# An MLP with SiLU and its gradients on one core: the last stores waited for on GpSimd, the first loads ahead of the entry barrier's arrival, and a warm-up that reads one broadcast column

## The chip, the cores and the metric

The kernel runs on one core of one Trainium2 chip. Times are device microseconds (us) of single executions. The span is the time from the first to the last instruction in the trace; the time was 1.7 to 1.9 us longer than the span in every run, and what fills that difference lies outside the trace. No run of this study was marked slow (the granted clock listed for each is 0.999 or 1.0), so all runs are compared.

## The reference

An MLP with SiLU, and its gradients; bfloat16 in and out, S = 2048, D = 640, F = 1536.

```python
def _fwd_reference(x, w1, w2):
    h = jnp.einsum("bsd,df->bsf", x, w1)
    h = _silu(h)
    return jnp.einsum("bsf,fd->bsd", h, w2)

def reference(x, w1, w2, grad_out):
    _out, _vjp = jax.vjp(_f, x, w1, w2)      # _f: _fwd_reference
    _grads = _vjp(grad_out)
    return (_out, *_grads)                   # out, grad x, grad w1, grad w2
```

## The kernel before

Six matmul stages follow each other on TensorE. The change touches only the two ends of the program.

At the start, each engine arrives at an entry barrier (a drain that adds to a semaphore), and then waits for GpSimd's release. A hook that edits the instruction list at the end of the build moves the first instructions between the arrival and the wait, so that they don't wait for the barrier:

```python
def start_before_entry_wait(nc, names):
    def move(nc):
        ...
            gate = next(
                k for k, i in enumerate(entry)
                if i.engine == engine and isinstance(i, mybir.InstEventSemaphore)
            )
            ...
            for i in reversed(moved):
                entry.insert(gate, i)
    nc.at_finalize(move)
```

Those instructions are a memset, 18 warm-up matmuls on the tile it fills, and the first loads. `x_nat` goes through ten TensorE transposes; `w1_nat` arrives in five row blocks of 384 KB (the first in two halves, one issued by SyncE and one by ScalarE), and the first matmuls consume it in that order. Warm-up matmuls are there because TensorE starts at half clock here: in the profile below, matmuls of 256 columns start 213 ns apart until 5.67 us and 109 ns apart after it. With 4 warm-up matmuls instead of 19, they became fast at 8.49 us instead of 4.33 (one profile each, in the experiments).

```python
NWARM = 18
...
warm = cpool.tile([P, P], dt_in, name="warm")
early = [nc.vector.memset(warm[:], 1.0)]
...
for i in range(NWARM):
    early.append(nc.tensor.matmul(wp[:, 0:P], lhsT=warm[:], rhs=warm[:], start=True, stop=True))
ident = cpool.tile([P, P], dt_in, name="ident")
make_identity(nc, ident[:])                       # on GpSimd, for the transposes
...
early += [load_x(nc.sync, 0), load_x(nc.scalar, 1)]
early += [load_w1(0, slice(0, F // 2)), load_w1(0, slice(F // 2, F), nc.scalar)]
early += [load_w1(k) for k in range(1, 3)]
for k in range(3, DT):
    load_w1(k)
...
def h_first(xT, aT, ghT):                         # the first stage
    pe_x(xT)                                      # ten transposes and their copies
    ...
    for dt_ in range(DT):                         # row block dt_ of w1: 12 matmuls of 256 columns
        for pair in range(NPAIR):
            h_pair_mm(hs[0][pair], pair, dt_, xT, halves[0])
    ...                                           # then 60 more for the second half of the columns
```

At the end, the last tile of the gradient of w1 is computed and stored in two pieces (384 and 128 columns), and another hook makes SyncE's wait for the last store the last of its waits:

```python
def wait_for_last_store_last(nc, name):
    def move(nc):
        ...
        late = [w for w in waits if w.id in lanes]
        waits = late + [w for w in waits if w.id not in lanes]
        end[at] = copy.replace(end[at], sync_info=mybir.SyncInfo(on_wait=waits, on_update=[]))
    nc.at_finalize(move)
```

After this wait, the exit sequence follows: all engines arrive, GpSimd gathers and releases them, GpSimd drains, clears the semaphores and drains, all arrive again, and GpSimd gathers and releases a second time.

## Time and profile before

| | before |
|---|---|
| time, median of 3 runs (range) | 320.86 us (320.43 to 321.17) |
| span of the profiled run | 318.9 us |
| last of the first loads that TensorE waits for ends | 7.69 us |
| last update of the last store, to the end of the span | 0.775 us |

First, the page of the profile: the busy line (share of the span), and the chain of work that ended last.

```profile
PE 314.2 (99%) x1516; PEld 150.7 (47%) x1544; DVE 102.7 (32%) x182; ACT 76.8 (24%) x139; POOL 0.7 (0%) x6
...
PE 96%; DMA 2%; issue 1%; SPq 0%; DVE 0%; DVEq 0%
PE hp L302 32%; PE hp L286 16%; PE hp L391 16%; PE hp L440 15%; PE hp L204 12%; PE hp L233 3%; DMA w_nat<-in_w_dram 2%; PE hp L421 1%; SPq L173 0%; SPq L170 0%; DVE g L432 0%; DVEq L432 0%; SPq L468 0%
```

TensorE is the bound, and only the load of w1 stands beside it in the chain, with 2%.

Second, the timeline of the first 8 us. Its columns are start and length in us, engine (SPq and ACTq are the sequencers that issue DMAs), line, operation and count; the bracket is idle time before the group and what ended it.

```profile
0.09 0.39 SPq L170 DMA_DIRECT2D x_nat<-in_x_dram  x1
0.21 0.38 ACTq L170 DMA_DIRECT2D x_nat<-in_x_dram  x1
...
0.28 0.17 DVE L143 MEMSET warm<- 128x128 bf16 x1 [0.28 <-issue]
...
0.50 2.10 PE L147 MATMUL wp<-warm 128*128 128x128 bf16 x18 [0.50 <-DVE warm L143]
0.54 2.31 SPq L173 DMA_DIRECT2D w_nat<-in_w_dram  x5
0.62 0.45 ACTq L173 DMA_DIRECT2D w_nat<-in_w_dram  x1
...
2.59 1.25 PE L195 MATMUL tp<-ident,x_nat 128*128 128x128 bf16 x10
...
3.79 4.45 PE L233 MATMUL hp<-xT,w_nat 128*128 128x256 bf16 x27
5.00 0.88 PEld L233 LDWEIGHTS <-w_nat 128*128 128x128 bf16 x6 [0.25 <-DMA w_nat<-in_w_dram]
6.18 1.21 PEld L233 LDWEIGHTS <-w_nat 128*128 128x128 bf16 x12 [0.30 <-DMA w_nat<-in_w_dram]
...
7.73 0.33 PEld L233 LDWEIGHTS <-w_nat 128*128 128x128 bf16 x4 [0.35 <-DMA w_nat<-in_w_dram]
```

TensorE's weight loader (PEld) waits for w1 three times, 0.25 to 0.35 us each, and not again after 7.73 us. The matmuls lose less by it: the first of these waits delays none of them, and the other two make one matmul each late, by 0.18 us at 6.18 us and by 0.23 us at 7.74 us (gaps between starts of 294 and 342 ns instead of 109).

Third, how fast TensorE runs in that stretch: three windows of 1.5 us, with TensorE's busy time, the number of matmuls, the granted clock, the DMA engines' share and GB/s.

```profile
5.00:6.50 1.50, 1.48 (x11) 1.00 0.84 287
6.50:8.00 1.50, 1.43 (x14) 1.00 1.08 387
8.00:9.50 1.50, 1.50 (x17) 1.00 1.07 189
```

A matmul of 256 columns starts every 213 ns at half clock and every 109 ns at full clock, so 7 or 14 of them start in a full window; the count also takes in those that are still running at its edges. The clock column says 1.00 throughout, although the starts are 213 ns apart until 5.67 us: the clock record in the trace file begins only where full clock is granted, at 5.66 us here, and the column takes what lies before it for full clock.

Fourth, the sequencers' instructions at the end, listed by source line (minimum, median and maximum ns; first and last start).

```profile
L479 POOLq DRAIN  x3: 34/78/386, 1.0 to 318.7; - x3
L479 SPq DRAIN  x3: 7/7/13, 318.2 to 318.5; - x3
...
L479 PEldq EVENT_SEMAPHORE  x2: 51/51/51, 318.4 to 318.9; - x2
L479 POOLq EVENT_SEMAPHORE_RANGE_CLEAR  x1: 96/96/96, 318.5 to 318.5; - x1
```

Apart from GpSimd's first drain, at 1.0 us, the instructions in these lines start after the last store has landed, at 318.15 us. The trace's record of instructions and semaphore updates gives the order:

```
318.147  last update of the last store's semaphore
318.164  SyncE drain (its wait for that store is over)
318.233  SyncE drain, arrives at the exit barrier
318.265  GpSimd gathers          318.344  GpSimd releases
318.429  GpSimd drain (78 ns)    318.536  GpSimd clears the semaphores (96 ns)    318.661  GpSimd drain (34 ns)
318.739  GpSimd gathers          318.818  GpSimd releases
318.871  TensorE's last wait, 51 ns: end of the span at 318.922
```

### The profile page before, as it was taken

How to read it: one execution, taken by the hardware profiler on the slowest of the kernel's cores; microseconds unless marked ns; L12 is line 12 of the kernel's file. 1: busy time of each engine (PE TensorE's matmuls, PEld its weight loads, DVE VectorE, ACT ScalarE, POOL GpSimd, SP SyncE). 2: the span in 40 equal slices, each digit the busy share in tenths (PEclk: the TensorE clock that was granted, in tenths of full speed). 3: DMA queues.
4: the chain of work that ended last, by engine and by line, in shares of the span. 5: the costliest groups of instructions: out<-in, count | busy, mean ns of one | idle time of the engine just before them, and what ended most of it. 6: DMA issues, size and time to landing. Idle time of an engine off the chain costs nothing.

```text
span 318.9 us, 3632 instructions
## 1 busy us (share of the span) xinstructions
PE 314.2 (99%) x1516; PEld 150.7 (47%) x1544; DVE 102.7 (32%) x182; ACT 76.8 (24%) x139; POOL 0.7 (0%) x6
## 2 busy tenths in 40 slices
PE   9999999999999999999999999999999999999996
PEld 7854444444444444444444444444444444444443
DVE  1494641477410187710147741000000100001001
ACT  2691000644201354311064420111100001001100
POOL 0000000000000000000000000000000000000000
PEclk9999999999999999999999999999999999999999
DMA  8999999999999866492544089919999999996111
GB/s 268 311 177 222 216 266 255 313 270 304 260 232 342 201 191 174 144 299 82 164 120 128 0 268 265 210 38 290 222 258 255 228 214 339 229 311 216 38 39 45
DMA packets 147233, 67.02 MB, mean 210 GB/s; under 512 B 113937, under 2 KB 146705, under 8 KB 147217
## 3 DMA queue, kind: packets, MB, share of 16 engines
q1 hardware_dynamic: 146928, 66.43, 83.0%
q10 hardware_dynamic: 288, 0.36, 0.3%
q8 instruction: 12, 0.20, 0.3%
q14 instruction: 5, 0.03, 0.0%
HBM read 9.18 MB, written 28.97 MB: 120 GB/s over the span
## 4 chain that ended last, share of the span: by engine, by line
PE 96%; DMA 2%; issue 1%; SPq 0%; DVE 0%; DVEq 0%
PE hp L302 32%; PE hp L286 16%; PE hp L391 16%; PE hp L440 15%; PE hp L204 12%; PE hp L233 3%; DMA w_nat<-in_w_dram 2%; PE hp L421 1%; SPq L173 0%; SPq L170 0%; DVE g L432 0%; DVEq L432 0%; SPq L468 0%
## 5 line engine op out<-in xcount | busy, mean ns | idle before, releaser
L286 PE MATMUL hp<-goT,w2T 128*128 128x512 bf16 x239 | 56.8, 379 | 0.1
L302 PE MATMUL hp<-ghT,w1T 128*128 128x512 bf16 x235 | 52.2, 379 | 0.3
L302 PE MATMUL hp<-aT,w_nat 128*128 128x512 bf16 x234 | 52.1, 379 | 0.3
L391 PE MATMUL hp<-a_blk,go_nat 128*128 128x512 bf16 x235 | 51.7, 379 | 0.3
L440 PE MATMUL hp<-gh_blk,x_nat 128*128 128x512 bf16 x219 | 48.2, 379 | 0.3
L204 PE MATMUL hp<-xT,w_nat 128*128 128x512 bf16 x174 | 43.4, 379 | 0.3
L310 ACT ACTIVATE oT<-hp 128x512 bf16<-128x512 f32 x24 | 14.5, 604 | 106.8 <-PE hp L302 106.8
L302 PEld LDWEIGHTS <-w1T 128*128 128x128 bf16 x240 | 23.5, 98 | 28.3
L391 PEld LDWEIGHTS <-go_nat 128*128 128x128 bf16 x240 | 23.5, 98 | 28.3
L286 PEld LDWEIGHTS <-w2T 128*128 128x128 bf16 x240 | 23.5, 98 | 28.3
L302 PEld LDWEIGHTS <-w_nat 128*128 128x128 bf16 x240 | 23.5, 98 | 28.1
L293 DVE SCALAR_TENSOR_TENSOR ghT<-ghT,hp 128x512 bf16<-128x512 bf16 x48 | 32.5, 681 | 7.3 <-PE hp L286 7.3
L440 PEld LDWEIGHTS <-x_nat 128*128 128x128 bf16 x224 | 21.9, 98 | 26.4
L312 DVE CAST oT<-hp 128x512 bf16<-128x512 f32 x16 | 11.1, 691 | 72.2 <-PE hp L302 67.7
L213 ACT ACTIVATE aT<-hp 128x512 bf16<-128x512 f32 x36 | 21.5, 597 | 30.4 <-PE hp L204 30.4
L204 PEld LDWEIGHTS <-w_nat 128*128 128x128 bf16 x180 | 17.6, 98 | 21.3
L220 DVE SCALAR_TENSOR_TENSOR ghT<-aT,v 128x512 bf16<-128x512 bf16 x36 | 24.6, 684 | 0.2
L219 DVE TENSOR_SCALAR v<-t 128x512 bf16<-128x512 f32 x36 | 15.4, 426 | 26.7 <-ACT t L217 26.7
L217 ACT ACTIVATE t<-hp 128x512 f32<-128x512 f32 x36 | 21.3, 592 | 0.0
L451 DVE CAST g<-hp 128x512 bf16<-128x512 f32 x7 | 4.8, 691 | 47.0 <-PE hp L440 34.5
L401 DVE CAST g2T<-hp 128x512 bf16<-128x512 f32 x7 | 4.8, 692 | 46.1 <-PE hp L391 46.1
L399 ACT ACTIVATE g2T<-hp 128x512 bf16<-128x512 f32 x8 | 4.8, 597 | 47.0 <-PE hp L391 47.0
(28 smaller groups left out, 77.3 us busy)
## 6 DMA issues: line engine op xcount, KB each, us to landing
aT_scr<-aT SPq DMA_DIRECT2D x4, 1536.0 KB, 6.3
ghT_scr<-ghT SPq DMA_DIRECT2D x4, 1536.0 KB, 8.2
out_dram<-o_sb SPq DMA_DIRECT2D x8, 640.0 KB, 3.3
oT_scr<-oT SPq DMA_DIRECT2D x4, 640.0 KB, 3.6
go_nat<-in_grad_out_dram SPq DMA_DIRECT2D x4, 640.0 KB, 8.3
gxT_scr<-oT SPq DMA_DIRECT2D x4, 640.0 KB, 4.7
w_nat<-in_w_dram SPq DMA_DIRECT2D x1, 1920.0 KB, 11.1
x_nat<-in_x_dram SPq DMA_DIRECT2D x3, 640.0 KB, 7.2
```

What stands on the lines that cost most here:

```text
L204: nc.tensor.matmul(hp[:], lhsT=w1_nat[:, dt_, ft * P:(ft + 1) * P], rhs=xT[:, dt_, :], start=(dt_ == 0), stop=(dt_ == DT - 1),)
L213: nc.scalar.activation(aT[:, ft, :], hp[:], ACT.Silu)
L217: nc.scalar.activation(t[:], hp[:], ACT.Tanh, scale=0.5)
L219: nc.vector.tensor_scalar(out=v[:], in0=t[:], scalar1=-0.5, scalar2=0.5, op0=ALU.mult, op1=ALU.add)
L220: nc.vector.scalar_tensor_tensor(out=ghT[:, ft, :], in0=aT[:, ft, :], scalar=1.0, in1=v[:], op0=ALU.subtract, op1=ALU.mult)
L286: nc.tensor.matmul(gp[:], lhsT=w2T[:, dt_, ft * P:(ft + 1) * P], rhs=goT[:, dt_, :], start=(dt_ == 0), stop=(dt_ == DT - 1),)
L293: nc.vector.scalar_tensor_tensor(out=ghT[:, ft, :], in0=ghT[:, ft, :], scalar=1.0, in1=gp[:], op0=ALU.add, op1=ALU.mult)
L302: nc.tensor.matmul(op_[:], lhsT=w_all[:, ft, dt_ * P:(dt_ + 1) * P], rhs=rhs_all[:, ft, :], start=(ft == 0), stop=(ft == FT - 1),)
L310: nc.scalar.activation(oT[:, dt_, :], op_[:], ACT.Copy)
L312: nc.vector.tensor_copy(out=oT[:, dt_, :], in_=op_[:])
L391: nc.tensor.matmul(gp[:], lhsT=go_nat[:, st, dt_ * P:(dt_ + 1) * P], rhs=a_blk[:, st, :], start=(st == 0), stop=(st == ST - 1),)
L440: nc.tensor.matmul(gp[:], lhsT=x_nat[:, st, dt_ * P:(dt_ + 1) * P], rhs=gh_blk[:, st, :], start=(st == 0), stop=(st == ST - 1),)
```

## The change

The intent was to save time at both ends. At the end, GpSimd waits for the two last stores instead of SyncE, and it does so after both gathers, so that only the clearing and the last release remain after the landing. At the start, the two x loads and the memset go ahead of each engine's arrival at the barrier. The warm-up tile shrinks to two columns, of which one is read 128 times (stride 0), so that the memset is shorter and the warm-up starts earlier; one more warm-up matmul fills the gain. Cut to its core:

```diff
@@ start_before_entry_wait @@
+            arrival = next(k for k, i in enumerate(entry) if i.engine == engine and isinstance(i, mybir.InstDrain))
...
             for i in reversed(moved):
-                entry.insert(gate, i)
+                if i.name not in first:
+                    entry.insert(gate, i)
+            for i in reversed(moved):
+                if i.name in first:
+                    entry.insert(arrival, i)
@@ wait_for_last_store_last becomes last_stores_end_on_pool @@
-        late = [w for w in waits if w.id in lanes]
-        waits = late + [w for w in waits if w.id not in lanes]
+        late = [w for lane in reversed(lanes) for w in waits if w.id == lane]
+        waits = [w for w in waits if w.id not in lanes]
         end[at] = copy.replace(end[at], sync_info=mybir.SyncInfo(on_wait=waits, on_update=[]))
+        pool = [i for i in end if i.engine == mybir.EngineType.Pool]
+        drain, gather, release, reset, clear, drain2, gather2, release2 = pool
...
+        reset = copy.replace(reset, sync_info=mybir.SyncInfo(on_wait=late, on_update=[]))
+        for i in (drain2, clear, reset, gather2):
+            end.insert(to, i)
@@ the kernel @@
-    NWARM = 18
+    NWARM = 19
...
-        warm = cpool.tile([P, P], dt_in, name="warm")
-        early = [nc.vector.memset(warm[:], 1.0)]
+        warm = cpool.tile([P, 2], dt_in, name="warm")
+        warm_pp = warm[:, 0:1].to_broadcast([P, P])
+        first = [nc.vector.memset(warm[:], 1.0)]
+        early = []
...
-            early.append(nc.tensor.matmul(wp[:, 0:P], lhsT=warm[:], rhs=warm[:], start=True, stop=True))
+            early.append(nc.tensor.matmul(wp[:, 0:P], lhsT=warm_pp, rhs=warm_pp, start=True, stop=True))
...
-        early += [load_x(nc.sync, 0), load_x(nc.scalar, 1)]
+        first += [load_x(nc.sync, 0), load_x(nc.scalar, 1)]
```

More of the change, by code (lines that the diff above doesn't have):

```diff
@@ L13, with start_before_entry_wait @@
 BF16 = mybir.dt.bfloat16
-def start_before_entry_wait(nc, names):
+def start_before_entry_wait(nc, first, names):
     def move(nc):
@@ L36, in move, with last_stores_end_on_pool @@
                     del home[k]
+            assert all(i.name in first for i in moved[: sum(i.name in first for i in moved)])
             for i in reversed(moved):
-                entry.insert(gate, i)
+                if i.name not in first:
[3 more added lines that the diff above has]
+                    entry.insert(arrival, i)
     nc.at_finalize(move)
-def wait_for_last_store_last(nc, name):
+def last_stores_end_on_pool(nc, names):
     def move(nc):
         blocks = nc.m.functions[0].blocks
-        store = next(i for b in blocks for i in b.instructions if i.name == name)
-        lanes = {u.id for u in store.sync_info.on_update}
+        stores = [next(i for b in blocks for i in b.instructions if i.name == name) for name in names]
+        lanes = [u.id for i in stores for u in i.sync_info.on_update]
         end = blocks[-1].instructions
@@ L53, in move @@
         waits = list(end[at].sync_info.on_wait)
-        late = [w for w in waits if w.id in lanes]
-        assert len(late) == 1 and not end[at].sync_info.on_update
-        waits = late + [w for w in waits if w.id not in lanes]
+        late = [w for lane in reversed(lanes) for w in waits if w.id == lane]
+        assert len(late) == len(names) and not end[at].sync_info.on_update
+        waits = [w for w in waits if w.id not in lanes]
         end[at] = copy.replace(end[at], sync_info=mybir.SyncInfo(on_wait=waits, on_update=[]))
+        pool = [i for i in end if i.engine == mybir.EngineType.Pool]
+        drain, gather, release, reset, clear, drain2, gather2, release2 = pool
+        assert gather2.sync_info.on_wait and not release2.sync_info.on_wait
+        assert all(i.sync_info is None or not i.sync_info.on_wait for i in (reset, clear, drain2))
+        closing = {i.name for i in (reset, clear, drain2, gather2)}
+        to = next(k for k, i in enumerate(end) if i.name == reset.name)
+        for k in reversed(range(len(end))):
+            if end[k].name in closing:
+                del end[k]
+        reset = copy.replace(reset, sync_info=mybir.SyncInfo(on_wait=late, on_update=[]))
+        for i in (drain2, clear, reset, gather2):
+            end.insert(to, i)
     nc.at_finalize(move)
@@ L180 @@
         nc.sync.dma_start_transpose(out=xT_next[:, :, HC:SC], in_=x2[HC:SC, :])
-        start_before_entry_wait(nc, {i.ins.name for i in early})
+        first = {i.ins.name for i in first}
+        start_before_entry_wait(nc, first, first | {i.ins.name for i in early})
         nc.scalar.activation(warm_a[:], warm[:, 0:1], ACT.Silu)
@@ L417 @@
                 if fc == NFC - 1 and dt_ == DT - 1:
+                    last_stores = []
                     for k, (lo, hi) in enumerate(((0, FC - P), (FC - P, FC))):
@@ L432 @@
                             nc.vector.tensor_copy(out=g1[:, lo:hi], in_=gp[:, lo:hi])
-                        last_store = nc.sync.dma_start(
+                        store = nc.sync.dma_start(
                             out=gw1_v[:, dt_, fc * FC + lo:fc * FC + hi], in_=g1[:, lo:hi]
                         )
-                    wait_for_last_store_last(nc, last_store.ins.name)
+                        last_stores.append(store.ins.name)
+                    last_stores_end_on_pool(nc, last_stores)
                     continue
```

## The prediction

> **What bounds the kernel now.** The page's busy table has TensorE at 314.2 of 318.9 us (99%), and the chain of waits puts 96% of the span on matmuls. From 7.74 to 316.3 us TensorE runs without a break worth naming. The change touches nothing there. Only two ends can move: the first 7.7 us and the 2.6 us after the last matmul.
>
> **The end.** In the record of instructions and semaphore updates, the last copy ends at 316.67, the last store is issued at 316.69 and its last update comes at 318.15. Then everything is in series: SyncE wakes (0.02) and passes two drains (0.09), GpSimd gathers and releases the exit barrier (0.08 + 0.10), drains, clears the semaphores and drains again (0.107 + 0.125 + 0.078 between starts), gathers and releases a second time (0.079 + 0.025), and the last engine leaves at 318.92: 0.775 us from landing to end.
>
> After the change SyncE does not wait for the two last stores. Its remaining five waits (0.065 us each) and drains end near 317.5, so both gathers and the first release run while the store is in flight, and GpSimd stands ready near 317.95, before the landing. What remains after it: wake 0.02, drain 0.107, clear 0.125, drain 0.078, release 0.025, last engine leaves 0.08: about 0.43 us. Gain **0.34 us**, all on the critical path. The landing itself does not change.
>
> **The start.** SyncE's drain is at 0.000 and its x load at 0.087; ScalarE's are at 0.132 and 0.207. Loads ahead of the drain can go at most 0.087 and 0.075 us earlier; some of that is the load's own issue time, so I count 0.05. The w1 loads' issue stays (the same instructions in another order). TensorE's three waits for w1 (0.25, 0.30, 0.35 us, timeline) show a stage bound by loads, the last at 7.69 us; the DMA engines are 0.92 to 0.99 busy from 2.5 to 7.7 us (windows), so an earlier x pulls forward the w1 data queued behind it by nearly the same. Gain **0.05 us** (0 to 0.09). Against it: ScalarE reaches the entry barrier about 0.09 us later, but nobody near the critical path waits for that (the identity is ready at 1.31, wanted at 2.59).
>
> The smaller memset (0.165 us now) ahead of the drain lets the warm-up start at about 0.40 instead of 0.50; 19 matmuls at 0.107 us end at about 2.45, when x lands. This shortens a hole that is off the critical path. I expect the stride-0 read to cost nothing[...]. No run here shows it yet. [...] the moment of full clock (5.66 us here) may shift between runs: noise of some 0.3 us.
>
> **Prediction.** 320.86 - 0.34 - 0.05 = about 320.45 us; range 320.1 to 320.85. Faster by over 2%: 0.5%; same: 99%; slower: 0.5%. The profiled span should shrink slightly more (to about 318.5), as its zero moves to the x load.
>
> **Shown right or wrong by:** landing to end of 0.40 to 0.48 us against 0.775; SyncE's last drains before the landing; warm-up pitch still 107 ns; x load as the first instruction; last w1 wait ending near 7.6.
>
> **What would make it wrong:** weight loads or matmuls slowed by the broadcast read, so that the warm-up delays the transposes; [...] GpSimd's drain slower when it carries the wait; the time being taken from a runtime stage that does not follow these ends.

## The result, and the profile after

| | before | after |
|---|---|---|
| time, median of 6 runs each (range) | 320.84 us (320.43 to 321.36) | 320.81 us (320.14 to 321.73) |
| span of the profiled run | 318.9 us | 319.4 us |
| first 512-column matmul of the second stage (profiled run) | 18.23 us | 19.01 us |
| from there to the end of the span | 300.69 us | 300.35 us |
| last update of the last store, to the end of the span | 0.775 us | 0.425 us |

The ratio is 1.0 with a 95% interval of 0.9982 to 1.0018: the same. A ratio is the mean time of one kernel's fast runs over that of the other's of the same rounds, so it is not quite the ratio of the medians quoted. The predicted gain of 0.39 us does not show, and the scatter of the runs is larger than it.

The page of after has the same bound:

```profile
PE 313.1 (98%) x1517; PEld 150.5 (47%) x1545; DVE 102.7 (32%) x182; ACT 76.8 (24%) x139; POOL 0.7 (0%) x6
...
PE 97%; DMA 2%; issue 1%; SPq 0%; DVE 0%; DVEq 0%
```

The sequencers' instructions at the end, as above: the last of SyncE's drains now starts at 318.4 us, 0.5 us ahead of the landing at 318.94; only the clear, GpSimd's drains and the last waits come after it.

```profile
L503 POOLq DRAIN  x3: 34/78/386, 1.2 to 319.2; - x3
L503 SPq DRAIN  x3: 7/7/7, 318.1 to 318.4; - x3
...
L503 PEldq EVENT_SEMAPHORE  x2: 51/51/51, 318.4 to 319.3; - x2
L503 POOLq EVENT_SEMAPHORE_RANGE_CLEAR  x1: 96/96/96, 319.1 to 319.1; - x1
```

The record of after has both gathers and the first release in front of the landing:

```
318.185  SyncE drain, arrives    318.217  GpSimd gathers    318.296  GpSimd releases    318.549  GpSimd gathers
318.645  GpSimd's wait for the first of the two stores is over
318.936  last update of the last store's semaphore
318.961  GpSimd drain (78 ns)    319.067  clear (96 ns)     319.192  drain (34 ns)      319.256  GpSimd releases
319.310  TensorE's last wait, 51 ns: end of the span at 319.361
```

The timeline of the first 8 us:

```profile
0.00 0.40 SPq L191 DMA_DIRECT2D x_nat<-in_x_dram  x1
0.12 0.39 ACTq L191 DMA_DIRECT2D x_nat<-in_x_dram  x1
0.15 0.06 DVE L163 MEMSET warm<- 128x2 bf16 x1
...
0.38 2.21 PE L168 MATMUL wp<-warm 128*128 128x128 bf16 x19 [0.38 <-DVE warm L163]
0.65 2.23 SPq L194 DMA_DIRECT2D w_nat<-in_w_dram  x5
0.77 0.34 ACTq L194 DMA_DIRECT2D w_nat<-in_w_dram  x1
...
2.43 1.22 PE L217 MATMUL tp<-ident,x_nat 128*128 128x128 bf16 x10
...
3.63 1.47 PE L255 MATMUL hp<-xT,w_nat 128*128 128x256 bf16 x12
```

The x loads are issued 0.09 us earlier, the memset takes 60 ns instead of 165, and the warm-up starts at 0.38 instead of 0.50. But the first two w1 loads are issued at 0.65 and 0.77 us instead of 0.54 and 0.62. The record shows why: SyncE's drain takes 117 ns and ScalarE's 145 ns when they follow the issue of a DMA, where they took 7 and 8 ns in front of it, in the profile of before. The loads behind these lose less: the second and third row blocks are issued 0.05 and 0.04 us later than before, at 1.04 and 1.51 us. In this run one row block of w1 landed late (7.17 us against 6.14), and TensorE stood from 5.1 to 7.2 us:

```profile
5.00:6.50 1.50, 0.11 (x1) 1.00 0.92 330
6.50:8.00 1.50, 0.79 (x8) 1.00 1.29 389
8.00:9.50 1.50, 1.50 (x16) 1.00 1.26 148
```

The ends can be separated without any timing noise. From the first 512-column matmul of the second stage to the end of the span TensorE never waits for anything but itself, and this stretch is the same in every profile to 0.01 us: 300.68 to 300.70 us in three profiles with the old end, and 300.34 to 300.35 us in eleven with the new end. So the new end is worth 0.35 us, and "the start" of any timed run is its span less 300.69 or 300.345 us (spans of timed runs are given to 0.1 us). The question is what happened to the start.

### The profile page after: what moved, and what is told of

The parts are those of the page before. It is cut to its first block, busy times and chain, and to the rows that moved or that the text cites. A ratio compares the mean times of both kernels' runs of the same rounds, so it can differ in the third digit from the quotient of the medians.

```text
span 319.4 us, 3634 instructions
## 1 busy us (share of the span) xinstructions
PE 313.1 (98%) x1517; PEld 150.5 (47%) x1545; DVE 102.7 (32%) x182; ACT 76.8 (24%) x139; POOL 0.7 (0%) x6
## 4 chain that ended last, share of the span: by engine, by line
PE 97%; DMA 2%; issue 1%; SPq 0%; DVE 0%; DVEq 0%
PE hp L324 32%; PE hp L308 16%; PE hp L413 16%; PE hp L464 15%; PE hp L226 12%; PE hp L255 4%; DMA w_nat<-in_w_dram 2%; PE hp L444 1%; SPq L191 0%; SPq L194 0%; DVE g L455 0%; SPq L492 0%; DVEq L455 0%
## 5 line engine op out<-in xcount | busy, mean ns | idle before, releaser
L226 PEld LDWEIGHTS <-w_nat 128*128 128x128 bf16 x180 | 17.6, 98 | 21.2
```

The costliest lines, as they stand in the source:

```text
L226: nc.tensor.matmul(hp[:], lhsT=w1_nat[:, dt_, ft * P:(ft + 1) * P], rhs=xT[:, dt_, :], start=(dt_ == 0), stop=(dt_ == DT - 1),)
```

## The experiments

Three theories were set against each other at first. The scatter theory: the start is unchanged on average and its scatter hid the gain. The start-costs theory: the start loses what the end gains. The absorbed theory: what the runtime does after the program swallows the gain. All kernels below gave correct results. "Before" was run beside each group: 11, 9 and 11 runs on three chips.

### The changed kernel again (no edit)

> The changed kernel once more, unaltered. Scatter theory (the end is 0.35 us shorter, the start is unchanged on average, and the 6 + 6 runs so far only hid that under run-to-run scatter of the first loads): about 0.35 to 0.4 us below before. Start-costs theory (the w1 loads go out 0.11 to 0.15 us later, and the start loses on average what the end gains): the same as before, within 0.15. Absorbed theory (the runtime's own closing stage swallows the gain of the end): the same as before, and time minus span about 0.35 larger than for before.

Measured: 321.09 us median (319.89 to 322.61, 6 runs) against 321.11; ratio 1.0 (0.9972 to 1.0029). Its start ran from 17.65 to 20.35 us. The profile fell on a slow one: TensorE waited 0.99 us for the first row block of w1, until 4.76 us (the last engine's part of that load landed at 4.71), and then ran at half clock until 9.90 us. The windows of this profile show it:

```profile
5.00:6.50 1.50, 1.50 (x9) 1.00 0.94 315
6.50:8.00 1.50, 1.50 (x9) 1.00 1.02 398
8.00:9.50 1.50, 1.50 (x9) 1.00 1.56 193
```

TensorE is busy all the time, yet shows 9 matmuls in each window where a window at full clock shows 16: the starts are 213 ns apart. The second stage began at 20.39 us. This added a fourth theory, the clock theory: a wait at an unlucky moment keeps TensorE at half clock for several us more (here until 9.90 us, against 5.67 us in the profile of before).

### Only the end

```diff
 # the changed kernel with start_before_entry_wait, warm tile, memset, NWARM and x loads of before
-        first += [load_x(nc.sync, 0), load_x(nc.scalar, 1)]
+        early += [load_x(nc.sync, 0), load_x(nc.scalar, 1)]
```

> Only the end of the change: GpSimd waits for the two last stores; start, warm-up and memset as before. Scatter theory: 0.35 us below before, with 0.42 to 0.43 us from last landing to end in the profile. Start-costs theory: also 0.35 below before. Absorbed theory: equal to before, although the profile shows the shorter end.

Measured: 320.45 us median (320.28 to 321.26, 6 runs) against 321.11; ratio 0.9978 (0.9958 to 0.9998), 0.424 us from landing to end. The time less the span is 1.80 us, as for before (1.78). The mean is 0.62 us below before: the end's 0.35, and for the rest starts that happened to be shorter. The gain of the end reaches the time, and the absorbed theory falls for this part of the change.

### Only the loads and the memset ahead of the arrival

```diff
 # before, with the new start_before_entry_wait
-        early = [nc.vector.memset(warm[:], 1.0)]
+        first = [nc.vector.memset(warm[:], 1.0)]
...
-        early += [load_x(nc.sync, 0), load_x(nc.scalar, 1)]
+        first += [load_x(nc.sync, 0), load_x(nc.scalar, 1)]
```

> Only the x loads and the memset (still 128 columns) ahead of the entry barrier's arrival; 18 warm-up matmuls on the full tile and the end as before. Scatter theory: within 0.1 us of before. Start-costs theory: 0.25 to 0.35 us above before, with the first w1 loads issued near 0.65 (SyncE) and 0.77 us (ScalarE) in the profile against 0.54 and 0.62.

Measured: 321.75 us median (320.66 to 322.74, 6 runs) against 321.11; ratio 1.0019 (0.9995 to 1.0042). The w1 loads are issued at 0.65 and 0.76 us, as the start-costs theory said, and the mean is 0.5 us above before, a little more than it said. The interval still touches 1.

### Only the warm-up

```diff
-    NWARM = 18
+    NWARM = 19
...
-        warm = cpool.tile([P, P], dt_in, name="warm")
+        warm = cpool.tile([P, 2], dt_in, name="warm")
+        warm_pp = warm[:, 0:1].to_broadcast([P, P])
...
-            early.append(nc.tensor.matmul(wp[:, 0:P], lhsT=warm[:], rhs=warm[:], start=True, stop=True))
+            early.append(nc.tensor.matmul(wp[:, 0:P], lhsT=warm_pp, rhs=warm_pp, start=True, stop=True))
```

> Only the warm-up: 128x2 tile read as one broadcast column, 19 matmuls; the memset after the arrival and everything else as before. Both theories: within 0.1 us of before, pitch of the warm-up 107 ns, weight loads about 152 ns. If the broadcast read or an earlier full clock is what costs, this one is 0.3 us above before.

Measured: 320.89 us median (320.43 to 321.65, 6 runs) against 321.11; ratio 0.999 (0.9969 to 1.001). The broadcast read cost nothing here: starts are 107 ns apart with it, as without it.

### The change without its loads-first part

```diff
 # the end-only kernel above, with the warm-up edit above
```

> The change without its loads-first part: new end and broadcast warm-up of 19, x loads and memset after the arrival as before. Scatter theory: like the changed kernel, 0.35 us below before. Start-costs theory (putting the x loads ahead of the arrival is what costs): 0.35 us below before, and 0.3 to 0.5 us below the changed kernel of the same call.

Measured: 320.40 us median (320.24 to 320.93, 5 runs) against 320.69; ratio 0.999 (0.9977 to 1.0003). The mean is 0.42 us below the changed kernel of the same call (below).

### The first row block of w1 ahead of the arrival as well

```diff
-        early += [load_w1(0, slice(0, F // 2)), load_w1(0, slice(F // 2, F), nc.scalar)]
+        first += [load_w1(0, slice(0, F // 2)), load_w1(0, slice(F // 2, F), nc.scalar)]
```

> The changed kernel with the two halves of the first w1 row block also ahead of the arrival, so that the engine's drain no longer holds them: issue near 0.46 us (SyncE) and 0.57 us (ScalarE) instead of 0.65 and 0.77. If the later issue of w1 is what the start costs: 0.3 to 0.5 us below the changed kernel of the same call. If it is scatter or the clock: the same as the changed kernel. The entry barrier then closes later (about 1.2 us), the identity is ready near 1.9 us, still before x at 2.4.

Measured: 320.53 us median (320.34 to 321.14, 5 runs) against 320.69; ratio 0.9994 (0.998 to 1.0007). The two loads are issued at 0.46 and 0.55 us. The mean is 0.31 us below the changed kernel of the same call.

### Fillers for TensorE while it waits

```diff
+            for i in range(8):
+                nc.tensor.matmul(wp[:, 0:P], lhsT=warm_pp, rhs=warm_pp, start=True, stop=True)
             for k, (tp, (lo, hi)) in enumerate(zip(tps, slices)):
```

> The changed kernel with 8 more warm-up matmuls between the transposes and the first matmul on w1, where TensorE waits for w1 (0.2 us in one profile, 1.3 us in another). Clock theory (in some runs [...] full clock comes 3.4 us later, at 9.9 us instead of 3.5 to 6.5, and the run is 1.3 to 2 us longer): the slow tail goes, no run over 1.2 us above the fastest, mean 0.2 to 0.4 us below the changed kernel of the same call. If the tail comes from late loads alone: the same spread as the changed kernel, mean equal or up to 0.2 us above.

Measured: 320.79 us median (320.22 to 321.19, 5 runs) against 320.69; ratio 0.9998 (0.9983 to 1.0012). The build placed the eight ahead of the transposes, not after them, so they lengthen the warm-up to 3.2 us and move the transposes back by 0.7 us. No run is more than 1 us above the fastest; the mean is 0.20 us below the changed kernel, at the low edge of what the clock theory expected.

### The changed kernel a third time

> The changed kernel a third time, to compare with on the same chip. Scatter theory: 0.35 to 0.4 us below before. Start-costs theory: equal to before within 0.2 us, and above the kernel with only the new end and warm-up.

Measured: 320.87 us median (320.21 to 321.88, 5 runs) against 320.69; ratio 0.9996 (0.9981 to 1.0011). The profile again has TensorE idle for 0.98 us ahead of its first matmul on w1 at 4.84 us, and matmuls at 213 ns until 8.41 us; the second stage began at 19.66 us. The mean is 0.13 us above before of the same call, as the start-costs theory expected; the scatter theory missed.

### The change without loads-first, again

> New end and broadcast warm-up, x loads after the arrival, once more: 0.3 to 0.4 us below before, no run more than 1.2 us above its fastest. It is the best candidate so far, and should beat before by about 0.1%.

Measured: 320.60 us median (320.39 to 321.32, 6 runs) against 321.16; ratio 0.9981 (0.9959 to 1.0002). No run over 1 us above its fastest. The mean is 0.61 us below before, more than expected. Its profile has full clock from 4.33 us; the wait in the first window (TensorE busy for 0.67 of 1.50 us) did no harm to it, since the clock had risen already; the next two windows count 16 matmuls each:

```profile
5.00:6.50 1.50, 0.67 (x7) 1.00 0.94 338
6.50:8.00 1.50, 1.50 (x16) 1.00 1.11 377
8.00:9.50 1.50, 1.50 (x16) 1.00 1.16 198
```

### TensorE left idle, loads untouched

```diff
 # the kernel just above
-    NWARM = 19
+    NWARM = 4
```

> The same with 4 warm-up matmuls instead of 19, so that TensorE idles some 1.6 us more before x lands; no load is touched. Clock theory (idle TensorE ahead of and at the first w1 wait [...] that costs time at the start): mean 0.2 to 0.6 us above the 19-matmul version of this call, some runs a microsecond or more longer, and often the matmuls on w1 still at 213 ns after 6.5 us. Loads theory (only the landing of w1 sets the start): equal to the 19-matmul version within 0.15.

Measured: 321.16 us median (320.11 to 322.88, 6 runs) against 321.16; ratio 0.9996 (0.9964 to 1.0028). The mean is 0.55 us above the 19-matmul version of the same call, with a standard error of 0.43, so the means alone decide nothing. In its profile all row blocks of w1 landed early (the third at 7.24 us, against 7.69 for before), but TensorE kept half clock until 8.49 us:

```profile
5.00:6.50 1.50, 1.50 (x8) 1.00 0.97 308
6.50:8.00 1.50, 1.50 (x9) 1.00 1.01 378
8.00:9.50 1.50, 1.50 (x14) 1.00 1.20 215
```

The second stage began at 19.41 us. Landing plus what was left to compute at full clock would have allowed it near 17.9: ScalarE's half of the first row block landed last, at 5.50 us, with 114 matmuls of 109 ns left, and the second block (5.78 us, 108 left) and the third (96 left) give 17.6 and 17.7. This is an estimate from those numbers. So in this run the late clock, with no load touched, cost more than a microsecond, and the theory that only the landing of w1 sets the start falls.

### The first row block of w1 ahead of the arrival, again

> The changed kernel with the first w1 row block also ahead of the arrival, once more. If the later issue of w1 made the long waits: again no run with a start over 19.4 us, mean start 18.4 (span 318.7, time 320.6). If the first sample was luck: 3 in 10 runs over 19.4, mean start 18.9.

Measured: 320.85 us median (320.51 to 320.97, 6 runs) against 321.16; ratio 0.9984 (0.9963 to 1.0004). No start over 19.4 us; mean start 18.55 us.

### Fillers, again

> The changed kernel with 8 filler matmuls, once more. Clock theory: no run with a start over 19.4 us, mean start 18.5 (time 320.7). If the first sample was luck: 3 in 10 runs over 19.4, mean start 18.9.

Measured: 320.83 us median (320.12 to 321.36, 6 runs) against 321.16; ratio 0.9986 (0.9963 to 1.0009). No start over 19.4 us; mean start 18.62 us. At 3 slow starts in 10, six runs without one would come by luck in 12% of cases, so each of these two repeats says little by itself.

### All runs together

The start (span less 300.69 or 300.345 us) of every timed run whose span is known. With spans to 0.1 us, the 19.41 us of the short warm-up's profile falls just under the limit here.

| kernel | runs | mean start | longest | runs of 19.4 us or more | time less span |
|---|---|---|---|---|---|
| before | 31 | 18.65 | 20.51 | 3 | 1.78 |
| only the end | 6 | 18.45 | 19.15 | 0 | 1.80 |
| only the warm-up | 6 | 18.51 | 19.21 | 0 | 1.78 |
| end and warm-up | 11 | 18.48 | 19.25 | 0 | 1.77 |
| only loads and memset first | 6 | 19.21 | 20.21 | 3 | 1.80 |
| the whole change | 17 | 18.81 | 20.35 | 4 | 1.89 |
| the whole change, w1's first block first too | 11 | 18.48 | 18.85 | 0 | 1.87 |
| the whole change, fillers | 11 | 18.57 | 19.15 | 0 | 1.88 |
| end and warm-up, 4 matmuls | 6 | 19.09 | 20.75 | 2 | 1.79 |

The four kernels with the x loads after the arrival and a full warm-up have a mean start of 18.58 us over 54 runs (standard error 0.07); the two with only the x loads ahead have 18.92 over 23 runs (0.16). Without the runs of 19.4 us and more, the means are 18.48 and 18.50. So the whole difference sits in a tail: 7 of 23 runs against 3 of 54 (chance of this by luck about 0.006, with the limit of 19.4 chosen after the first eight kernels had run; with 19.2 it would be 7 against 6, and 0.04). The chips are not the reason: in the two calls that hold both kinds, it is 6 of 17 against 1 of 37. Only two of these ten slow runs have a profile, the second and third of the changed kernel; both show the late clock, and what made the other eight slow is not known. Adding the w1 block or the fillers brings it to 0 of 22.

## Why the prediction was right or wrong

The time on record, 320.45 us, and the measured 320.81 both lie in the stated range, and "same" was right. That is mostly luck: 320.81 is inside because the range reached to 0.01 us below the time before, and "same" was safe for so small a change. The gain that the number was made of did not come, so the sum has to be gone through term by term.

- **The end, 0.34 us: right.** Landing to end fell from 0.775 to 0.425 us, SyncE's last drain starts before the landing, and the end-only kernel turned it into time. The drain, clear and release on GpSimd took what they had taken before: from drain to clear 0.106 us, from clear to drain 0.125 and from the last release to TensorE's last wait 0.054, against 0.107, 0.125 and 0.053.
- **The broadcast read: right.** Pitch 107 ns, and the weight loads of the warm-up take 151 ns with a stride of 0 (the profile of after) and 152 ns with a stride of 1 (that of before).
- **"The w1 loads' issue stays (the same instructions in another order)": wrong.** This is the step that failed. The order mattered: the drains behind a DMA issue took 117 (SyncE) and 145 ns (ScalarE) in the profile of after, instead of 7 and 8 in that of before, so the first w1 loads go out 0.11 (SyncE) and 0.15 us (ScalarE) later.
- **"An earlier x pulls forward the w1 data queued behind it": not seen.** The first packet of x came at 1.01 to 1.04 us in the eight profiles with the loads ahead, and at 1.10 to 1.11 in the six without. But the last part of SyncE's x load landed at 2.51 us on average of eight profiles with, and at 2.53 in six without. Landings of single w1 blocks differ by a microsecond between runs of one kernel (the wait for the first block ended at 3.63, 4.76 and 4.84 us in the three profiles of the changed kernel), far more than what was to be gained. The three waits that the prediction reasoned from are also not TensorE's own but its weight loader's: the matmuls of before lost 0.42 us to them, not 0.90.
- **"Noise of some 0.3 us" for the moment of full clock: mis-sized.** The 512-column matmuls of the second stage began at 18.0 to 18.7 us where full clock came before 6.6 us and w1 was not late; where it came at 8.4 to 9.9 us, they began at 19.4 to 20.4. The 0.3 us was the author's estimate, with no run behind it.

  Eleven of the fourteen trace files hold the stretch of full clock, in a record that the views do not print: it begins at 3.50 to 6.54 us, in one at 9.91, and lasts 310.61, 314.03 or 317.44 us (314.03 in the profile of before, 317.44 in that of after), so the lengths are 3.41 us apart. What sets these steps was not shown.

  In the profile with full clock at 9.91 us, TensorE was idle for 0.38 us before the warm-up and for 0.99 us of waiting for w1, until 4.76 us. The third profile of the changed kernel and that of the short warm-up have no clock record. In the former, matmuls become fast at 8.41 us, after 0.37 us of idle time before the warm-up and a wait for w1 of 0.98 us, until 4.84; in the latter at 8.49 us, after 0.38 us before the warm-up, 1.64 us for want of warm-up matmuls, until 2.62, and 0.21 us of waiting for w1, until 4.08. Where full clock came at 5.66 us (before) and 3.50 us (after), TensorE had been idle for 0.50 and 0.38 us, all of it ahead of the warm-up. The matmul ends behind these figures are modelled. A long wait by itself did not make the clock late: the longest for the first row block, 1.56 us in the end-only profile, came with full clock at 4.02 us, just as the wait began. That idle time ahead of the rise delays it is the author's reading of these profiles; how much of it is needed was not shown.
- **A term that was not in the sum.** Every kernel with both the loads and the small memset ahead of the arrival has 1.87 to 1.89 us of time outside the span, all others 1.77 to 1.80. That takes 0.1 us of the gain. These kernels all have the new end too, and the one kernel with loads ahead and the old end has 1.80, so it may be the small memset, or the new end together with the loads ahead. The traces show nothing outside the program, and no experiment took this apart; it stays open.

The balance for the whole change against before, in means over all runs with known span: end -0.35, start +0.16 (standard error 0.2), outside the span +0.11, together -0.07 us, which is the difference of the mean times (321.05 against 321.12). Against the kernel that differs only in where the loads and the memset stand, the start is 0.33 us (0.2) longer. Such means are the best that these runs give: the ends are known to 0.01 us, the start only to some 0.2.

What is shown: the end's gain; the later issue of w1; that a late full clock cost over a microsecond (by the estimate for the short warm-up, 19.41 us against some 17.9), and that it came in three profiles where TensorE had been idle for 1.35 to 2.23 us in all ahead of it, with a wait for w1 of 0.21 to 0.99 us in that. That slow starts are more frequent with the x loads ahead is likely from the counts, with the reserve made there. What is only argued: that this idle time made the clock late, and that the later w1 and the earlier x, by lengthening TensorE's wait between them, are why the clock came late more often. Both remedies that shorten or fill that wait fit this (0 of 22), but w1's landings in single profiles scatter too much to prove it, and the longest wait for the first row block (1.56 us) came in a profile with the x loads after the arrival.

The best version measured is the new end with the broadcast warm-up and the loads left after the arrival: 0.9990 and 0.9981 of before in two calls, and a mean of 320.59 us over 11 runs, against 321.05 over 17 for the whole change and 321.12 over 31 for before. Neither interval excludes 1, but the 0.35 us of it at the end are seen in every profile. The new end alone is as good within the scatter: 0.9978, and a mean of 320.60 us over 6 runs.

## What to carry to other kernels

Work that waits for nothing but a barrier can be moved in front of the last wait of a program; that gain was exact here, 0.35 us, and showed in one profile. Moving a DMA issue in front of a barrier's arrival made the drain behind it longer here (117 and 145 ns instead of 7 and 8), so look at what that drain now holds back. When a change is worth tenths of a microsecond and the start of the kernel hangs on loads and on a TensorE that is still at half clock (here until 3.50 to 9.91 us), split the span at a point after which nothing waits, and compare distributions of the first part: a rise in rare slow starts looks like "no gain" in a median.
